# A fused infini-attention and MLP kernel whose hand-held order of 1,426 pieces of work is replaced by another

## The chip, the cores and the metric

The kernel runs on one core of one Trainium2 chip. The metric is the device time of one execution, in microseconds (us). The core has TensorE (PE in the profile), VectorE (DVE), ScalarE (ACT), GpSimd (POOL) and SyncE (SP, which here only issues DMAs). Each engine takes its instructions strictly in the order in which they stand in its queue; an instruction that waits for a semaphore holds up everything behind it on that engine.

## The reference

One transformer block on x of 2048 tokens by 640 features, in bfloat16: a layer norm, infini-attention with 32 heads of 20 features, a residual, a second layer norm, and an MLP with 1728 hidden features and SiLU, with a residual.

```
x = A_x
h  = x + A(layernorm(x))            # infini-attention
h2 = h + silu(layernorm(h) @ w1) @ w2

A(x):  q, k, v = x @ wq, x @ wk, x @ wv        # 32 heads x 20
  M = z = 0
  for s in range(4):                            # segments of 512 tokens
    p     = softmax(qs @ ks.T * 20**-0.5 + causal mask)
    a_dot = p @ vs
    a_mem = (phi(qs) @ M) / (phi(qs) @ z + 1e-6)    # phi(t) = t+1 if t > 0 else exp(t)
    out_s = g * a_mem + (1 - g) * a_dot             # g = sigmoid(beta)
    M, z  = M + phi(ks).T @ vs, z + sum(phi(ks))
  return concat(out_s) @ wo
```

## The kernel before

The work of the four segments is cut into 1,426 **tasks**, each a short run of instructions on one engine (a projection of a column block, one exp, one DMA). `build()` declares them all, `Graph.schedule()` puts them in one sequence, and they are emitted in that sequence into the engines' queues. A tracker follows who last wrote and read each buffer and sets the semaphore waits from that, so any sequence computes the same thing, and the sequence alone decides what an engine has next in its queue and what that has to wait for.

The sequence is a module-level table, `ORDER` (lines 356 to 460), a list of words of the form `name/engine:slots`. The name picks a task. The letter behind the slash picks the engine where a task may run on several: A is ACT, D is DVE, G is POOL, S is SP. The numbers behind the colon give the buffers that the task takes from the pools that it touches first, above all the **PSUM banks** (eight, 0 to 7): a score takes four neighbouring banks (`:4` is banks 4 to 7) or two, a V projection two, a projection or a part of the MLP one bank. A task that takes a bank waits for the last reader of what lay there. A `+` in the name of an exp makes one exp of 2048 columns out of two of 1024; `fill2` is a run of two matmuls on zeros, whose result nobody reads. What `schedule()` does with a word:

```
            name, _, slots = row.partition(":")
            name, _, eng = name.partition("/")
...
            t.eng = {"A": AC, "D": DV, "G": PO, "S": SP}[eng] if eng else list(t.engs)[0]
...
                    a.slot = slots.pop(0)
                    for k in range(a.slot, a.slot + a.size):
                        o = owner[a.pool][k]
                        assert o is None or o.users == 0, (name, a.pool)
```

The tasks by their names, with the line that shows up in the profile:

- **First norm**: n1_st, n1_r, n1_ap are statistics and normalisation of one block of 128 tokens; n1_tr4 to n1_tr15 are DMA transposes of the blocks of segments 1 to 3 into xT (L799, from SP); segment 0 goes over PE instead (L779).
- **Loads**: x0 to x14 (L576 ff.), the weights (L582); w_w1_0 to w_w1_4 are five pieces of w1.
- **Projections** (`declare_front`): pr (L867, in segment 0 also L872) into PSUM, qe is the copy of it to SBUF (L883, on ACT or DVE; the copies go into buffers that the trace calls w_sb in segment 0 and QK later). v00 to v03 are the V projections of the four 128-token blocks of segment 0 (L828, ten matmuls of 320 columns each), ve the copy into Vx (L842/L843), v10 to v13 those of segment 1. ex (L890) and pha, phb (L743 and others) make phi.
- **Virtual heads**: only four heads fit the rows of a 128-partition block at steps of 32, with 12 rows over in each step. Twelve small DMAs per segment, vt (L915), gather those rows of the q and k chunks into three more chunks, QKV (vt x0, x3, x6, x9 from chunks 0 to 2; the other eight from chunks 3 and 4). The scores of head groups 5, 6 and 7 read them. In segment 0 these copies are traced as w_sb<-w_sb. vp (of segments 1 and up) does the same for phi.
- **Scores** (L965): qk, row-tiled matmuls, four side by side, one for each head of a group of four, into four PSUM banks. Segment 0 is cut in halves of its queries: 0x1 to 0x3 are the first half of groups 0 to 3 on its own keys, packed into three scores, 4x1 to 4x3 that of groups 4 to 7 (4x3 is the one that the prediction calls the third score), 0y1 to 0y3 and 4y1 to 4y3 the second half on its own keys, 0ya to 7ya the second half of each group on the keys of the first. 0x1 and its like consist of a wide part and two narrow ones, 0x2 of two wide parts. 4x1 reads the virtual heads of group 5 beside group 4, 4x2 those of groups 5 and 6. qk8 to qk31 are segments 1 to 3. **Exps** (L977, ACT): e, named as their score. Masks mk (L988, POOL).
- **Attention output**: av (L1009, L1093), oe the copy of it, tn the transpose back (L1039, L1043, L1124), nm the division, ad the sum with the memory part, which together fill otok.
- **Memory**: kt (L1208) transposes phi(k), mz (L1226) multiplies it with V, ma (L1238) is the copy of the memory matrix Mz out of PSUM (ma00 the first one), mb copies the running matrix for the next segment.
- **Back** (`declare_back`): ot transposes otok into oT by DMA (L1265, from SP), wo0 to wo15 is the projection with wo (L1273), rs adds the residual (L1281), n2_ the second norm, h1 (L1308, tail L1302) the first MLP product by column blocks (h1_1_9 is block 9 of segment 1), th the tanh (L1317), s the rest of SiLU (L1323), h2 (L1350) the second product, o (L1363) the last residual, out (L1368) the store. bsel (L638) and zf (L649) are small preparations from beta on ACT.

PE works in two modes, whole-array matmuls (pr, v, mz, wo, h1, h2) and row- or column-tiled ones (qk, av, tn), and the order decides how often it changes.

Of the kernel before, what the change touches and what calls it, by code (L numbers as in the profile page):

```python
# [324 lines left out]
D = 640  # L325
# [31 lines left out]
epsg0:0 vpad0 zpad w2z/G:0 fill30:7 x0:0 w_q1:0 warm iota mt mta mtb mm7 x1:4 mm0 n1_st1/A:0,0 w_q0 w_q2 epsc sel  # L357
halfc n1_st0/D:5 n1_r0/G n1_r1/D n1_ap0:0 n1_tp0:4 n1_te0a/A:0 n1_ap1:1 n1_tp1:0 n1_te0b/A n1_te1b/D n1_te1a/A w_k0
re_wq1/D:0 pr010x:4 re_wq4/A re_wq2/D pr020x:2 qe020x/A:0 qe010x/A:0 re_wq3/D re_wq0/D pr000x:5 pr040x:6 w_k1
re_wk2/A:0 qe000x/A:0 re_wk1/D qe040x/A:0 pr011x:0 qe011x/A re_wk0/D pr001x:2 pr021x:5 qe001x/A qe021x/A x2:10,5  # L360
n1_st2/D:3 n1_r2/G qk0x10:0 pr030x:7 w_wv0:0 w_wv1 n1_st3/D:1 n1_r3/G e0x10:4 x4:2,1,11,3 qe030x/A:0 w_wo:0 beta
w_w1_0:0 e0x12 re_wk3/D pr031x:6 n1_ap2:2 re_wk4/D x8/S:6,7,8,9 n1_ap3:0 n1_tp2:0 n1_te2/D n1_st6:4 n1_tp3:4 n1_r6/G
n1_te3/A qe031x/D pr041x:7 qe041x/D qk0x20:0 e0x2+:6 pr030y:4 qe030y/D pr031y:5 qe031y/A pr041y:6 qe041y/A pr040y:7
qe040y/A vt02/S:0 vt011/S vt05/S vt08/S n1_st5:1 qk0x30:0 vt04/S mk0x1_0 mk0x1_256 n1_st4:5 n1_r5/G n1_ap5:1 e0x3+:0
n1_ap6:2 pr000y:4 qe000y/D lsc0 vt07/A pr021y:6 qe021y/D pr001y:5 qe001y/D pr011y:7 ex021:0 qe011y/D pr020y:1 n1_r4/D
mk0x3_0 qe020y/D mk0x3_256 vt010/A pr010y:6 qe010y/D vt00/A vt03/A vt06/S v03:2 ve03/D:0 ex001:1 mk0x3_384 mk0x2_0
v00:4 ve00/D qk0y10:0 e0y12:5 mk0x1_384 pha021:1 pha001:2 v01:6 e0y10 mk0y1_0 mk0x2_256 vt09/S phb021 vt01/S qk4x10:2
phb001 lsc1 n1_st7:7 e4x1+:2 vpad1 v02:0 ve01/D av0x:6 mk4x1_0 n1_ap4:3 n1_r7/G qk4x20:2 e4x2+:1 n1_tr5:0 mk4x1_256
mk4x1_384 ve02/D lsc2 lsc3 oe0x/D:0 mk4x2_0 mk4x2_256 av2x:7 ex041:1 oe2x/D:1 kt02:0 n1_tr6 mk0y1_256 mm2 kt00:1 v11:0
qk4x30:2 e4x30:3 pha011:0 ve11/D:1 tn0x:6 nm0x:3 e4x32 mk4x3_0 pha031:1 qk0ya0:0 mk4x3_256 n1_ap7:2 mk4x3_384 v12:6  # L370
e0ya+:4 w_w1_2 ve12/D av4x:4 oe4x/D:0 mz00:5 ma00/A:2,5 qk1ya0:0 e1ya2:0 tn2x:6 nm2x:0 av6x:7 oe6x/D:1 e1ya0 tn4x:6
nm4x:1 qk2ya0:2 kvz e2ya2:1 tn6x:7 mm3 nm6x:2 n1_tr4 v10:0 n1_st11:2 e2ya0 qk0y20:4 e0y2+:6 w_w1_3 w_w1_1 mk0y2_0
kg00/G:0 mk0y2_256 n1_tr7 v13:2 n1_r11/G qk3ya0:4 e3ya0:3 ve10/D n1_st9:6 n1_r9/D pha041:2 ex031:2 mm6 ve13/D ot1:0
wo1:0 n1_st8:3 e3ya2 ot0 ex011:0 wo0:2 rs1 n2_st1:0 mk0y1_384 w_w1_4 phb011 qk4ya0:4 e4ya0:2 n2_r1/D kg02/G e4ya2 rs0
n2_ap1:0 n2_st0:0 pr101:0 qe101/A:0 av0y:1 qk0y30:2 e0y3+:0 w_w2_0/S pr120:6 zf0 n2_r0/D oe0y/D:0 pr100:7 mk0y3_0
ex101:0 qk5ya0:2 n2_ap0:3 e5ya2:4 n2_tr1:0 phb041 qe100/D e5ya0 qe120/D:0 pr121:0 qe121/D qk4y10:4 mk0y3_256 tn0y:1
nm0y:3 e4y10:5 e4y12 mk0y3_384 n1_r8/D av2y:0 oe2y/D:1 qk6ya0:2 mk4y1_0 pha120:0 pr141:1 qe141/D:0 phb031 n2_tr0
h1_0_7_0:6 e6ya+:0 th0_7_0:0 s0_7_0:0 h1_0_12_0:0 th0_12_0:1 qk7ya0:1 e7ya+:1 kt01:0 w_w2_5 h1_0_4_0:7 tn2y:5 s0_12_0
h1_0_3_0:6 kg01/G mk4y1_256 n1_st10:1 th0_3_0:0 mk4y1_384 qvz h1_0_6_0:0 qk4y20:1 th0_4_0:1 nm2y:3 s0_4_0 mm4
h1_0_5_0:5 e4y2+:3 s0_3_0 pr110:7 qe110/D:0 th0_5_0:1 qk4y30:1 pr140:6 th0_6_0:0 e4y32:6 mk4y2_0 e4y30 w_w2_1/S  # L380
# [1046 lines left out]
```

## Time and profile before

| | before |
|---|---|
| median of 3 runs | 296.9 us (296.9 to 297.67) |
| the profiled execution: span | 296.3 us |
| its busy time, PE | 282.1 us (95%) |
| DVE / ACT / POOL | 222.2 / 217.3 / 140.0 us |
| instructions | 7,415 |

The page of the profile is one execution; its span runs from the first to the last instruction, 0.6 us less than the median of the runs. A view by windows gives, for each stretch, PE, PEld (weight loads), DVE, ACT and POOL busy time with the number of instructions, then the granted clock of PE, the busy share of the DMA engines and the GB/s. A timeline row reads: start, duration, engine, line, operation, output<-input, shape; xN joins N instructions alike that stand together, and the square bracket gives the idle time ahead of it and what ended it. In the view of waits a row gives the waiting instruction, the releaser, then the total, the number and the longest of such waits. Some matmul records are missing from the trace, so that a gap of about 0.2 us between matmuls need not be idle time.

### The profile page before, as it was taken

To read this page: it belongs to the slowest core of one execution; us is meant where nothing else is said; L and a number is where in the kernel's file an instruction comes from. 1 tells how busy PE (TensorE), PEld (TensorE's weight loads), DVE (VectorE), ACT (ScalarE), POOL (GpSimd) and SP (SyncE) were. 2 spreads that over 40 slices of the span, in tenths; PEclk is the share of its full clock that TensorE was granted. 3 is DMA by queue.
4 is the path that set the end of the run, shared out by engine and by line. 5 is a ranking of instruction groups with operands and counts; after the bars stand their busy time and mean duration, and the time that the engine had idled before them with its cause. 6 is when DMAs were issued, how large, how long until landed. Compare 5 with 4: busy or idle time off the path is not lost.

```text
span 296.3 us, 7415 instructions
## 1 busy us (share of the span) xinstructions
PE 282.1 (95%) x2968; PEld 167.6 (57%) x2991; DVE 222.2 (75%) x506; ACT 217.3 (73%) x266; POOL 140.0 (47%) x257
## 2 busy tenths in 40 slices
PE   7897889999999999999999999999999999999997
PEld 5675445555665455566643545465665457764575
DVE  3897799778979779899698967759967688626522
ACT  4884989999999899998879999788759750014400
POOL 6237735645566477646526646455476620200000
PEclk9999999999999999999999999999999999999999
DMA  7956973803953221255433400144171023220002
GB/s 243 367 173 105 173 133 71 221 18 75 189 94 74 53 60 22 40 109 106 104 96 61 66 1 2 27 76 87 22 99 32 0 61 74 68 67 25 22 22 91
DMA packets 49922, 25.40 MB, mean 86 GB/s; under 512 B 39504, under 2 KB 48048, under 8 KB 49888
## 3 DMA queue, kind: packets, MB, share of 16 engines
q1 hardware_dynamic: 47804, 22.69, 36.2%
q10 hardware_dynamic: 2084, 2.23, 2.4%
q8 instruction: 24, 0.39, 0.5%
q14 instruction: 10, 0.08, 0.1%
HBM read 10.41 MB, written 2.62 MB: 44 GB/s over the span
## 4 chain that ended last, share of the span: by engine, by line
PE 78%; DVE 8%; DMA 6%; issue 2%; ACT 2%; SPq 1%; POOL 1%; DVEq 0%; ACTq 0%
PE ps_all L1350 19%; PE ps_all L1308 17%; PE ps_all L867 12%; PE ps_all L965 7%; PE ps_all L1273 6%; PE ps_all L828 5%; PE ps_all L1009 5%; DMA x_tok<-in_A_x_dram 3%; DMA xT<-xn_rot 2%; ACT PT L977 2%; PE ps_all L1039 1%; DVE stt L743 1%; PE ps_all L1093 1%; DMA w_sb<-w_sb 1%; PE ps_all L1226 1%
## 5 line engine op out<-in xcount | busy, mean ns | idle before, releaser
L977 ACT ACTIVATE PT<-ps_all 128x1024 bf16<-128x1024 f32 (+1 forms) x120 | 153.2, 1310 | 16.9 <-PE ps_all L965 15.7
L988 POOL TENSOR_SCALAR_AFFINE_SELECT PT<-PT 128x512 bf16<-128x512 bf16 x128 | 81.6, 648 | 59.2 <-ACT PT L977 56.9
L1350 PE MATMUL ps_all<-w_sb,sT 128*128 128x320 bf16 (+2 forms) x462 | 64.9, 295 | 0.0
L1308 PE MATMUL ps_all<-hT,w_sb 128*128 128x512 bf16 (+1 forms) x315 | 61.0, 336 | 1.2 <-issue 0.6
L1317 ACT ACTIVATE th<-ps_all 128x512 f32<-128x512 f32 (+2 forms) x70 | 34.1, 505 | 35.3 <-PE ps_all L1308 31.2
L1350 PEld LDWEIGHTS ps_all<-w_sb,sT 128*128 128x128 bf16 x462 | 43.2, 98 | 18.3 <-issue 1.8
L1323 DVE SCALAR_TENSOR_TENSOR sT<-th,ps_all 128x512 bf16<-128x512 f32 (+2 forms) x70 | 37.9, 561 | 17.8 <-ACT th L1317 16.9
L1308 PEld LDWEIGHTS ps_all<-hT,w_sb 128*128 128x128 bf16 x325 | 29.9, 98 | 25.3 <-issue 3.5
L764 POOL TENSOR_TENSOR rst<-rst,eps_c 128x1 f32<-128x1 f32 x32 | 18.3, 576 | 24.4 <-DVE rst L758 23.1
L743 DVE BATCH_NORM_STATS2 stt<-x_tok 128x6 f32<-128x320 bf16 x62 | 27.2, 481 | 1.1 <-DMA x_tok<-in_A_x_dram 0.7
L1363 DVE SCALAR_TENSOR_TENSOR x_tok<-ps_all,x_tok 128x640 bf16<-128x640 f32 (+3 forms) x18 | 13.3, 745 | 16.7 <-PE ps_all L1350 16.6
L1071 POOL TENSOR_TENSOR otok<-on 128x320 bf16<-128x320 bf16 x24 | 19.0, 797 | 11.7 <-DVE on L1063 11.7
L1273 PE MATMUL ps_all<-wo_sb,oT 128*128 128x320 bf16 x160 | 23.8, 299 | 0.0
L884 DVE CAST QK<-ps_all 128x512 bf16<-128x512 f32 x23 | 15.7, 688 | 9.1 <-PE ps_all L867 8.9
L1063 DVE TENSOR_TENSOR on<-ps_all,rd 128x640 bf16<-128x640 f32 x24 | 19.8, 824 | 0.9
L828 PE MATMUL ps_all<-wv_sb,xT 128*128 128x320 bf16 x120 | 18.3, 299 | 1.1 <-DMA xT<-xn_rot 0.9
L1273 PEld LDWEIGHTS ps_all<-wo_sb,oT 128*128 128x128 bf16 x160 | 15.0, 98 | 7.2 <-issue 1.8
L867 PE MATMUL ps_all<-xT,wkr 128*128 128x512 bf16 x67 | 16.9, 379 | 1.2 <-issue 0.8
L867 PE MATMUL ps_all<-xT,wqr 128*128 128x512 bf16 x70 | 17.3, 380 | 0.4 <-issue 0.2
L1009 PE MATMUL ps_all<-PT,Vx 128*32 128x512 bf16 (+3 forms) x384 | 16.4, 301 | 0.1
L843 DVE CAST Vx<-ps_all 128x640 bf16<-128x640 f32 x15 | 12.3, 818 | 5.4 <-PE ps_all L828 5.3
L770 DVE TENSOR_SCALAR xn_rot<-x_tok,mvt,rst 128x640 bf16<-128x640 bf16 x32 | 14.9, 475 | 1.7 <-POOL rst L764 1.0
(106 smaller groups left out, 337.4 us busy)
## 6 DMA issues: line engine op xcount, KB each, us to landing
w_sb<-in_B_w_dram SPq DMA_DIRECT2D x5, 432.0 KB, 6.3
w_sb<-in_B_w_dram SPq DMA_DIRECT2D x3, 480.0 KB, 4.6
x_tok<-in_A_x_dram SPq DMA_DIRECT2D x2, 640.0 KB, 9.7
out_dram<-x_tok ACTq DMA_DIRECT2D x8, 160.0 KB, 1.8
out_dram<-x_tok SPq DMA_DIRECT2D x7, 160.0 KB, 1.9
x_tok<-in_A_x_dram SPq DMA_DIRECT2D x3, 320.0 KB, 3.4
QKV<-QK SPq DMA_DIRECT2D x12, 72.0 KB
wo_sb<-in_A_wo_dram SPq DMA_DIRECT2D x1, 800.0 KB, 10.4
```

The costliest lines, as they stand in the source:

```text
L743: T.add(DV, lambda e, hh=hh: e.bn_stats(out=stt[:, s, 6 * hh:6 * hh + 6], in_=xb[:, 320 * hh:320 * hh + 320]), reads=R((xa, xsub)), writes ...
L828: fns.append(lambda e, c=c, hh=hh: e.matmul(bank(ps, hh)[:, 0:320], lhsT=xT_[:, c, 128 * i:128 * i + 128], rhs=wv_sb[:, c, 320 * hh:320 * ...
L867: fns = [lambda e, kc=kc: e.matmul(bank(ps)[:, lo:hi], lhsT=wt[:, kc, c, :], rhs=xT_[:, kc, lo:hi], start=(kc == 0), stop=(kc == NC - 1)) ...
L965: fns.append(lambda e, j=j, o=o, r=r, q0=q0, q1=q1, qa=qa, ka=ka: e.matmul(ps_all[:, o:o + q1 - q0], lhsT=ka[32 * r:32 * r + DH, 128 * j:1 ...
L977: T.add(AC, lambda e: e.activation(out=pt[:, pta.slot, q0:q0 + nq, 0:width], in_=sc3[:, b0:b0 + nq, 0:width], func=ACT.Exp, scale=SCALE), ...
L988: T.add(PO, lambda e: e.affine_select(out=v, in_=v, pattern=[[0, 4], [1, 128]], compare_op=ALU.is_ge, fill=0.0, base=0, channel_multiplier ...
L1009: fns.append(lambda e, j=j, r=r, h=h, pa=pa, pt=pt, co=co, q0=q0, ji=ji: e.matmul(bank(po)[32 * r:32 * r + 32, q0:hi], lhsT=Vx[:, vx.slot, ...
L1273: fns.append(lambda e, c=c, hh=hh: e.matmul(bank(ps, hh)[:, 0:320], lhsT=oT[:, c, 128 * i:128 * i + 128], rhs=wo_sb[:, c, 320 * hh:320 * h ...
L1308: fns = [lambda e, c=c: e.matmul(bank(ps)[:, lo:hi], lhsT=w1_sb[:, c, 128 * f:128 * f + 128], rhs=hT[:, c, lo:hi], start=(c == 0), stop=(c ...
L1317: T.add(AC, lambda e: e.activation(out=th[:, tha.slot, lo:hi], in_=bank(ps)[:, lo:hi], func=ACT.Tanh, scale=0.5), reads=R((ps, [0])), writ ...
L1323: T.add(DV, lambda e: e.scalar_tensor_tensor(out=sT[:, f, lo:hi], in0=th[:, tha.slot, lo:hi], scalar=1.0, in1=bank(ps)[:, lo:hi], op0=ALU. ...
L1350: fns.append(lambda e, f=f, t0=t0, fr=fr, hh=hh, n=n: e.matmul(bank(pa, hh)[:, 0:n], lhsT=sT[:, f, t0:t0 + 128], rhs=w2_sb[:, fr, c0 + 320 ...
```

## The change

Only the table `ORDER` changes. Its first loads and norms stay nearly as they were; behind them the words stand in a new order, with other engines and other buffers for some. All 1,426 tasks are in both tables. Of the 381 tasks on PE, 198 stand at the same place in PE's queue. 21 copies go from DVE to ACT and 13 from ACT to DVE; 16 small tasks go from DVE to POOL and 11 back. 32 DMA issues (14 vt, 12 vp, two pieces of w2, x12, three stores) go from SP to ACT, 9 from ACT to SP. 40 exps are whole 2048-column ones in both. PE's mode changes are 195 before and 192 after. The filler of two matmuls that closed the program stands ahead of h1_2_4 instead, and the last piece of output has 192 columns instead of 128.

One line of the table around the V projections of segment 0, before and after:

```
-qe020y/D mk0x3_256 vt010/A pr010y:6 qe010y/D vt00/A vt03/A vt06/S v03:2 ve03/D:0 ex001:1 mk0x3_384 mk0x2_0
...
+n1_ap6:0 n1_ap7:1 vt02/A n1_ap5:2 vt04/S v03:2 v00:0 lsc0 lsc1 kvz ve03/D:1 vt01/A vt010/S lsc2 vt00/S mk0x3_0
```

On PE, at the V projections of segment 0 (L828, v03 first), before. The scores (L965) among them are 0y1 behind the first two, and 4x1; the L1093 rows are the attention output av0x, and the last row is score 4x2:

```order
L828 MATMUL ps_all<-wv_sb,hT 128x320 x20
L965 MATMUL ps_all<-w_sb 128x256 x4
L965 MATMUL ps_all<-w_sb 128x128 x8
L828 MATMUL ps_all<-wv_sb,hT 128x320 x10
L965 MATMUL ps_all<-w_sb 128x256 x4
L965 MATMUL ps_all<-w_sb 128x128 x8
L828 MATMUL ps_all<-wv_sb,hT 128x320 x10
L1093 MATMUL ps_all<-PT,Vx 32x256 x4
L1093 MATMUL ps_all<-PT,Vx 32x128 x4
L1093 MATMUL ps_all<-PT,Vx 32x256 x4
L1093 MATMUL ps_all<-PT,Vx 32x128 x4
L965 MATMUL ps_all<-w_sb 128x256 x8
```

The same place of PE after:

```order
L965 MATMUL ps_all<-w_sb 128x256 x4
L965 MATMUL ps_all<-w_sb 128x128 x8
L828 MATMUL ps_all<-wv_sb,hT 128x320 x40
L965 MATMUL ps_all<-w_sb 128x256 x8
L1093 MATMUL ps_all<-PT,Vx 32x256 x4
L1093 MATMUL ps_all<-PT,Vx 32x128 x4
```

Score 0y1 now stands ahead of all four V projections, these follow one another, and score 4x2 (the row of 8) comes ahead of 4x1, which stands behind four pairs of L1093 (av0x and av2x).

On ACT at the same place before; the exps (L977) are the two halves of 0y1, then 4x1 and 4x2 whole, and the DMAs (L915) are four of the twelve virtual-head copies:

```order
L915 DMA w_sb<-w_sb 8x2x1024
L890 ACTIVATE ex<-w_sb 128x512
L915 DMA w_sb<-w_sb 8x2x1024
L915 DMA w_sb<-w_sb 12x3x1024 x2
L890 ACTIVATE ex<-w_sb 128x512
L977 ACTIVATE PT<-ps_all 128x1024 x2
L977 ACTIVATE PT<-ps_all 128x2048 x2
```

And after, from behind four copies of projections (L883) on:

```order
L977 ACTIVATE PT<-ps_all 128x1024
L915 DMA w_sb<-w_sb 12x3x1024
L977 ACTIVATE PT<-ps_all 128x1024
L915 DMA w_sb<-w_sb 8x1x1024
L638 ACTIVATE bsel<-beta_bc 128x32
L915 DMA w_sb<-w_sb 8x2x1024
L649 ACTIVATE zf<-beta_bc 128x32
L842 ACTIVATE Vx<-ps_all 128x32x20
L890 ACTIVATE ex<-w_sb 128x512 x2
L977 ACTIVATE PT<-ps_all 128x2048
L890 ACTIVATE ex<-w_sb 128x512
L977 ACTIVATE PT<-ps_all 128x2048
```

The two exps of 0y1 now come first, with DMA issues between them and the two whole exps, of which 4x2's is the first; one of the copies of V (L842) and zf (L649) lie between.

On SP, at the transposes of segment 1 (L799; n1_tr4 and n1_tr7 are the last two of them) and the loads of w1 (L582), before:

```order
L582 DMA w_sb<-in_B_w_dram 128x1728
L799 DMA_TRANSPOSE xT<-xn_rot 128x5x128
L582 DMA w_sb<-in_B_w_dram 128x1728 x2
L799 DMA_TRANSPOSE xT<-xn_rot 128x5x128
L1265 DMA_TRANSPOSE oT<-otok 128x5x128 x2
```

And after:

```order
L1208 DMA_TRANSPOSE phiKt<-phiK 128x4x128
L582 DMA w_sb<-in_B_w_dram 128x1728
L1208 DMA_TRANSPOSE phiKt<-phiK 128x4x128
L799 DMA_TRANSPOSE xT<-xn_rot 128x5x128 x2
L1265 DMA_TRANSPOSE oT<-otok 128x5x128 x2
L582 DMA w_sb<-in_B_w_dram 128x1728
```

Only one piece of w1 stands ahead of the two transposes now; the two that stood between them come behind.

More of the change, by code (lines that the diff above doesn't have):

```diff
@@ L356 @@
 ORDER = """
[L357 removed]
+epsg0:0 vpad0 zpad w2z/G:0 fill30:7 x0:8 w_q1:0 warm iota mt mta mtb mm7 x1:7 mm0 n1_st1/A:0,0 w_q0 w_q2 epsc sel
 halfc n1_st0/D:5 n1_r0/G n1_r1/D n1_ap0:0 n1_tp0:4 n1_te0a/A:0 n1_ap1:1 n1_tp1:0 n1_te0b/A n1_te1b/D n1_te1a/A w_k0
[L359 to L360 removed]
@@ L371 @@
[L371 to L380, printed above, removed]
@@ new lines @@
+nm6x:3 n1_tr4 v10:0 ve10/D qk0y20:4 e0y2+:4 mzc0 n1_st9:1 v13:2 qk3ya0:4 ve13/D e3ya0:1 ot1:0 e3ya2 wo1:0 mk0y1_0
+mk0y1_256 mk0y1_384 ot0 qk4ya0:2 mzc1 e4ya2:2 mk0y2_0 w_w1_1 pha011:2 phb011 n1_r8/D mk0y2_256 rs1 n2_st1:6 n2_r1/D
+e4ya0 kg02/G kt01:1 w_w1_3 wo0:6 rs0 av0y:1 qk0y30:2 oe0y/D:0 e0y3+:5 n2_st0:4 pr101:6 w_w1_4 qe101/D:0 ex101:0 tn0y:1
+pr120:0 qk5ya0:2 e5ya2:3 n2_ap1:0 pr100:7 n2_tr1:0 qe120/D:0 n2_r0/G n2_ap0:1 mk0y3_0 mk0y3_256 mk0y3_384 n2_tr0 e5ya0
+pr121:0 ex031:2 qe100/D nm0y:2 qk4y10:4 e4y10:6 qe121/D e4y12 av2y:1 qk6ya0:2 e6ya+:0 w_w2_0/S n1_st10:6 pr141:0
```

180 lines of the change are left out of this document (93 added, 87 removed).

## The prediction

> **What bounds the kernel now.** I read the page first, then PE's waits, then windows by stage, then the timeline of the one stage that has room.
>
> ```profile
> span 296.3 us, 7415 instructions
> ...
> PE 282.1 (95%) x2968; PEld 167.6 (57%) x2991; DVE 222.2 (75%) x506; ACT 217.3 (73%) x266; POOL 140.0 (47%) x257
> ...
> PEclk9999999999999999999999999999999999999999
> ```
> PE is busy 95% at full granted clock all through. The change keeps every computation (one filler is placed elsewhere), so it can win only idle time of PE. Where is that idle time? PE's waits, all of them by cause (total, times, longest):
>
> ```profile
> PE ps_all L965 <- DMA w_sb<-w_sb: 1.5, 1, 1.5
> PE ps_all L872 <- DVE wqr L695: 1.2, 1, 1.2
> PE ps_all L620 <- DVE zpad L597: 1.1, 1, 1.1
> ...
> PE ps_all L779 <- DVE xn_rot L770: 0.9, 2, 0.6
> PE ps_all L965 <- DVE otok L1138: 0.9, 1, 0.9
> PE ps_all L828 <- DMA xT<-xn_rot: 0.9, 1, 0.9
> ```
> 1.1 (filler), 1.2 and 0.9 belong to the first loads and norms, whose order ahead of the projections stays. The other three large ones are 3.3 us. The windows say where they are (columns: PE, PEld, DVE, ACT, POOL busy):
>
> ```profile
> 20.00:48.00 28.00, 23.98 (x304) 15.18 (x303) 24.07 (x58) 21.47 (x23) 17.43 (x33) 1.00 0.69 128
> 48.00:80.00 32.00, 30.55 (x415) 17.97 (x418) 26.55 (x69) 31.73 (x42) 16.58 (x29) 1.00 0.52 112
> 80.00:150.00 70.00, 68.77 (x800) 40.54 (x805) 59.24 (x135) 62.91 (x74) 42.90 (x77) 1.00 0.38 74
> ```
> Between 20 and 48 us PE idles 4.0 us. Between 48 and 80 us it idles 1.45 us and ACT only 0.27: there **ACT sets the pace**, and PE can come earlier only if ACT does. From 80 us PE's waits, asked for alone, name two that are more than issue, 0.4 and 0.3 us:
>
> ```profile
> PE ps_all L1226 <- DVE x_tok L1281: 0.4, 1, 0.4
> PE ps_all L1308 <- DVE rd L1057: 0.3, 1, 0.3
> ```
> So the time is decided before 80 us, and in 20 to 48 us above all.
>
> **Stage 20 to 48 us.** These rows are PE's, ACT's and two DMAs' of that stage:
>
> ```profile
> 22.29 2.88 PE L828 MATMUL ps_all<-wv_sb,hT 128*128 128x320 bf16 x20
> 25.11 0.40 PE L965 MATMUL ps_all<-w_sb 20*128 20x256 bf16 x12
> 28.47 0.40 PE L965 MATMUL ps_all<-w_sb 20*128 20x256 bf16 x12 [1.50 <-DMA w_sb<-w_sb]
> 33.23 0.40 PE L965 MATMUL ps_all<-w_sb 20*128 20x256 bf16 x12
> 42.68 1.53 PE L828 MATMUL ps_all<-wv_sb,xT 128*128 128x320 bf16 x10 [0.85 <-DMA xT<-xn_rot]
> 47.85 1.03 PE L867 MATMUL ps_all<-xT,wkr 128*128 128x512 bf16 x4 [0.16 <-DVE stt L743]
> ```
> ```profile
> 18.28 0.93 ACT L883 ACTIVATE w_sb<-ps_all 128x256 bf16<-128x256 f32 x3
> 19.12 1.88 ACT L977 ACTIVATE PT<-ps_all 128x2048 bf16<-128x2048 f32 x1
> 21.36 3.34 ACTq L915 DMA_DIRECT2D w_sb<-w_sb  x3
> 24.75 0.63 ACT L890 ACTIVATE ex<-w_sb 128x512 bf16<-128x512 bf16 x1 [2.76 <-DVE Vx L843]
> 28.92 1.88 ACT L977 ACTIVATE PT<-ps_all 128x2048 bf16<-128x2048 f32 x1 [1.43 <-PE ps_all L965]
> 31.30 1.88 ACT L977 ACTIVATE PT<-ps_all 128x2048 bf16<-128x2048 f32 x1 [0.50 <-PE ps_all L965]
> 41.88 1.88 ACT L977 ACTIVATE PT<-ps_all 128x2048 bf16<-128x2048 f32 x1 [0.21 <-PE ps_all L965]
> 44.59 1.02 ACT L977 ACTIVATE PT<-ps_all 128x1024 bf16<-128x1024 f32 x1 [0.84 <-PE ps_all L965]
> ```
> ```profile
> 23.78 0.78 SPq L915
> 24.60 3.73 DMA w_sb<-w_sb
> ...
> 35.73 6.91 DMA xT<-xn_rot
> ```
> Before, the score of group 4 (28.47) waits 1.50 us for the last virtual-head copy, issued at 24.60 and landed 3.73 later. The change puts all four V projections and one early score (qk0y1) ahead of it, and score 4x2 ahead of 4x1. I follow it by hand.
>
> Step 1: qk0y1 needs ACT's copies of the projections. ACT ends its exp at 19.12 + 1.88 = 21.0, then has one ex (0.63) and four copies, which start 0.27 apart (18.28: three in 0.93, one is 0.38); the third frees qk0y1 at about 22.8, the fourth ends at 23.05. PE loses 0.4 there. Step 2: one V projection takes (25.11 - 22.29)/2 = 1.4 less a switch, 1.36; the score and four of them end at 22.8 + 0.35 + 5.45 + 0.1 = **28.7**. Step 3: the virtual-head copies of the first three chunks become issuable at 23.05; three on SP at about 0.8 each end at 25.5, and landing takes 3.73 - 0.70 = 3.03 from the issue's end: 28.5. So 4x2 starts at 28.7 and **the 1.50 us wait goes**, with 0.2 us to spare. Step 4: what is late next is ACT. Before, one 1.88 us exp (28.92) ran beside PE's V projection and the second ended at 33.18; now both lie behind 28.7. 4x2's exp is 28.7 + 0.45 (28.92 - 28.47) = 29.15 to 31.03; 4x1 shares two PSUM banks with 4x2 (slots 4 and 2, four banks each), waits for that end, and its exp is 31.55 to 33.43. The third score starts at 33.5, where it started at 33.23: **0.25 late**. The early end of V is given back. Step 5: behind it both kernels run the same exps; moving the Mz copy from ACT to DVE takes away 0.3, and the V projection that now must wait for its PSUM pair costs about 0.3. The exp of 41.88 comes 0.3 late. Step 6: n1_tr4 and n1_tr7 now go ahead of two w1 loads on SP, so the 6.91 us landing shortens and the **0.85 us wait goes**; but the next score needs the banks of the 41.88 exp, which ended at 43.76, and ACT's idle before 44.59 was 0.84. Of that, the 0.3 is made up; wo0 then waits for the PSUM of exp 3ya2. The set of PE work done at 47.62 (0.22 ahead of the row at 47.85, whose first matmul's record is lost) is reached at about 47.85: **+0.25 us**. The 3.3 us of waits are nearly all replaced by ACT's chain.
>
> What a change of tiling mode costs:
>
> ```profile
> 101.46 1.24 PE L867 MATMUL ps_all<-xT,wqr 128*128 128x512 bf16 x5
> 102.63 0.40 PE L965 MATMUL ps_all<-QKV 20*128 20x512 bf16 x4
> 102.96 1.25 PE L867 MATMUL ps_all<-xT,wkr 128*128 128x512 bf16 x5
> ```
> Four row-tiled matmuls take 0.33 where one of 512 columns takes (1.24 - 0.38)/4 = 0.215: 0.11 a change. PE changes mode 195 times before and 192 after, all three fewer ahead of 48 us. [...] I take 0, since in this stage PE waits for ACT anyway.
>
> **Stage 48 to 80 us.** ACT loses one copy (qe101, now DVE's) and zf0, and gets ex031 (0.63): even. The early exp at 50 us does not help: tn0y is put ahead of score 4y1, PE reaches that later, and the exps behind are paced by it: **+0.1**.
>
> **From 80 us.** The filler of two matmuls moves from behind the last output to ahead of h1_2_4, on PE's path: 0.2 us (bounds 0 if PE waits there, 0.38 by its row). The last output part is 192 columns instead of 128: 0.36 for 0.29, **+0.07**.
>
> ```profile
> 293.44 0.36 DVE L1363 SCALAR_TENSOR_TENSOR x_tok<-ps_all,x_tok 128x192 bf16<-128x192 f32 x1 [0.89 <-PE ps_all L1350]
> 293.80 0.38 PE L620 MATMUL ps_all<-zpad 128*128 128x256 bf16 x2
> 294.00 0.29 DVE L1363 SCALAR_TENSOR_TENSOR x_tok<-ps_all,x_tok 128x128 bf16<-128x128 f32 x1 [0.20 <-PE ps_all L1350]
> ```
> Of the waits from 80 us the 0.3 (h1_1_9, whose bank was mz20's) goes, as mz20 is moved ahead; I leave the 0.4: **-0.3**. New waits there are unknown: 0 to +1.0 (a handful of 0.2 each, the size of those found now), taken as 0.
>
> **DMA issues.** 32 go from SP to ACT and 9 back. Covered, they cost nothing: the one at 190.42 took 0.72 inside an exp.
>
> ```profile
> 190.36 1.88 ACT L977 ACTIVATE PT<-ps_all 128x2048 bf16<-128x2048 f32 x1 [0.20 <-PE ps_all L965]
> 190.42 0.72 ACTq L915 DMA_DIRECT2D QKV<-QK  x1
> ```
> Uncovered they do: three at 21.36 took 3.34, and ACT idled 2.76 before 24.75. Nearly all new ones stand behind an exp of 1.0 to 1.9, so I take 0; bounds 0 and 23 x 0.72 = 17 of ACT.
>
> **The sum** against the profiled execution: +0.25 + 0.1 + 0.2 + 0.07 - 0.3 = +0.3 on 296.3. The median of the runs, 296.9, lies 0.6 above that span: **297.2 us**.
>
> **The rivals.** (a) *The late landings are the bound, and ACT follows.* If step 4's ACT chain is shorter than I make it (qk0y1 frees at 22.4, 4x2 at 28.3), 0.4 less there, 0.4 at step 5, none of the 0.25, and half of the 0.85 kept: about -1.6, **295.3**. For it: three waits of 3.3 us do go. Against: ACT's 0.27 us of idle from 48 to 80. [...] Chance 0.28. (b) *The landing is late after all.* Slower: place, score 4x2; it decides once the last copy lands after 28.7, since then both exps and everything to 80 us move with it, one for one. One further issue (0.8) and a landing 0.4 slower (3.4) make +1.2: **298.4**. Chance 0.18. (c) *ACT's issues block*: from 48 to 150 us thirteen of the moved ones stand on ACT; if three are uncovered at 0.72, +2.1: **299.3**. Chance 0.08. That the order has no effect at all is excluded: the queues stand as the table says.
>
> **Chances.** Forecast 0.46 (own range 296.3 to 298.1). A measurement of this kernel can tell 0.3%, 0.9 us, from no change. Faster by that is most of (a) and a little of the forecast: 0.30. Slower is (b), (c) and the forecast's upper end, where unknown waits from 80 us add: 0.28. The rest, 0.42, is within. The range 294.6 to 299.0 takes in the forecast, (b), and (a) with the mode changes' 0.3 and the 0.4 of the L1226 wait gained as well (295.3 - 0.7).
>
> **What would show it.** In the changed profile PE's waits must no longer name w_sb or xT DMAs; 4x2's score should start near 28.7 and the third at 33.5; ACT must be solid from 50 to 80 us; waits from 80 us should stay under 1 us. Wrong it is if 4x2 starts after 29.5 (b), if the third score starts before 33.0 (a), or if ACT shows idle time beside its own DMA issues (c).

## The result, and the profile after

| | before | changed |
|---|---|---|
| median | 296.9 us (296.68 to 297.67) | 301.31 us (300.23 to 303.26) |
| ratio to before | 1 | 1.0146, 95% interval 1.0103 to 1.0189 |
| profiled execution: span, granted clock | 296.3 us, 1.000 | 299.9 us, 0.994 |

The changed kernel is 1.5% slower; 297.2 us was predicted, and the range ended at 299.0. From the page of the changed kernel:

```profile
span 299.9 us, 7422 instructions
...
PE 287.5 (96%) x2991; PEld 168.8 (56%) x2991; DVE 218.3 (73%) x493; ACT 220.6 (74%) x274; POOL 140.6 (47%) x262
...
PEclk9999979999999999999999999999999999999999
```

PE's busy time is 5.4 us more than before though its work is nearly the same: 23 of its matmuls had no record before (2,968 of 2,991), and a slower clock stretches others here (v10 below takes 2.82 us at a granted clock of 0.50). In the sixth fortieth of the span (37.5 to 45 us) the clock's digit is 7; before, it was 9 all through. The windows (PE, PEld, DVE, ACT, POOL busy, granted clock, DMA share, GB/s) put that in the stage that the prediction worked through, and show that ACT is no longer solid behind it:

```profile
20.00:48.00 28.00, 23.51 (x290) 14.25 (x287) 21.32 (x52) 21.99 (x27) 17.40 (x33) 0.94 0.47 95
48.00:80.00 32.00, 31.06 (x422) 17.93 (x423) 25.88 (x62) 30.38 (x38) 15.67 (x31) 1.00 0.58 135
```

PE's waits by cause:

```profile
PE ps_all L965 <- ACT PT L977: 3.8, 7, 1.2
...
PE ps_all L1308 <- DMA hT<-xn_rot: 0.5, 1, 0.5
PE ps_all L965 <- DMA w_sb<-w_sb: 0.4, 1, 0.4
```

The wait for the virtual-head copies fell from 1.5 to 0.4 us and the one for xT is gone. In their place scores wait 3.8 us for ACT's exps, a cause that was not in the list before. PE's timeline of the stage (start, duration, and in brackets the idle time ahead):

```profile
22.34 0.40 PE L965 MATMUL ps_all<-w_sb 20*128 20x256 bf16 x12 [0.20 <-ACT w_sb L883]
22.67 5.61 PE L828 MATMUL ps_all<-wv_sb,hT 128*128 128x320 bf16 x40
28.72 0.40 PE L965 MATMUL ps_all<-w_sb 20*128 20x256 bf16 x8 [0.44 <-DMA w_sb<-w_sb]
...
31.10 0.40 PE L965 MATMUL ps_all<-w_sb 20*128 20x256 bf16 x12 [1.18 <-ACT PT L977]
...
33.48 0.40 PE L965 MATMUL ps_all<-w_sb 20*128 20x256 bf16 x12 [0.52 <-ACT PT L977]
...
37.80 0.40 PE L965 MATMUL ps_all<-w_sb 20*128 20x256 bf16 x8 [0.91 <-ACT PT L977]
...
40.40 2.82 PE L828 MATMUL ps_all<-wv_sb,xT 128*128 128x320 bf16 x10
...
43.56 1.53 PE L828 MATMUL ps_all<-wv_sb,xT 128*128 128x320 bf16 x10
...
48.14 1.52 PE L1273 MATMUL ps_all<-wo_sb,oT 128*128 128x320 bf16 x10 [0.34 <-ACT PT L977]
```

Up to 33.48 the stage runs as forecast. Then one V projection, v10 at 40.40, takes 2.82 us where its like at 43.56 takes 1.53. Nothing waits in it: PE's granted clock is 0.50 there, from 39.94 to 43.35 us (the windows are under e13).

### The profile page after: what moved, and what is told of

It is laid out like the page before. It is cut to its first block, busy times and chain, and to the rows that moved or that the text cites. A ratio compares the mean times of both kernels' runs of the same rounds, so it can differ in the third digit from the quotient of the medians.

```text
span 299.9 us, 7422 instructions
## 1 busy us (share of the span) xinstructions
PE 287.5 (96%) x2991; PEld 168.8 (56%) x2991; DVE 218.3 (73%) x493; ACT 220.6 (74%) x274; POOL 140.6 (47%) x262
## 4 chain that ended last, share of the span: by engine, by line
PE 75%; ACT 11%; DVE 5%; DMA 4%; issue 2%; SPq 2%; ACTq 0%
PE ps_all L1350 18%; PE ps_all L1308 16%; PE ps_all L867 11%; ACT PT L977 9%; PE ps_all L1273 7%; PE ps_all L965 7%; PE ps_all L828 5%; PE ps_all L1009 4%; PE ps_all L620 2%; DMA x_tok<-in_A_x_dram 2%; SPq L915 1%; DMA w_sb<-w_sb 1%; DMA hT<-xn_rot 1%; PE ps_all L1039 1%; ACT th L1317 1%
## 5 line engine op out<-in xcount | busy, mean ns | idle before, releaser
L977 ACT ACTIVATE PT<-ps_all 128x1024 bf16<-128x1024 f32 (+1 forms) x120 | 153.0, 1310 | 18.9 <-PE ps_all L965 17.6
L1308 PE MATMUL ps_all<-hT,w_sb 128*128 128x512 bf16 (+1 forms) x325 | 62.9, 337 | 0.5 <-DMA hT<-xn_rot 0.5
L828 PE MATMUL ps_all<-wv_sb,xT 128*128 128x320 bf16 x120 | 19.6, 313 | 0.5 <-DVE on L1063 0.2
L867 PE MATMUL ps_all<-xT,wkr 128*128 128x512 bf16 x75 | 18.7, 380 | 0.0
L867 PE MATMUL ps_all<-xT,wqr 128*128 128x512 bf16 x75 | 18.4, 380 | 0.0
L884 DVE CAST QK<-ps_all 128x512 bf16<-128x512 f32 x21 | 14.4, 686 | 4.6 <-PE ps_all L867 4.4
L1281 DVE TENSOR_TENSOR x_tok<-ps_all,x_tok 128x640 bf16<-128x640 f32 x16 | 13.0, 813 | 5.6 <-PE ps_all L1273 5.3
```

Of the source, the lines that this page charges most:

```text
L828: fns.append(lambda e, c=c, hh=hh: e.matmul(bank(ps, hh)[:, 0:320], lhsT=xT_[:, c, 128 * i:128 * i + 128], rhs=wv_sb[:, c, 320 * hh:320 * ...
L867: fns = [lambda e, kc=kc: e.matmul(bank(ps)[:, lo:hi], lhsT=wt[:, kc, c, :], rhs=xT_[:, kc, lo:hi], start=(kc == 0), stop=(kc == NC - 1)) ...
L977: T.add(AC, lambda e: e.activation(out=pt[:, pta.slot, q0:q0 + nq, 0:width], in_=sc3[:, b0:b0 + nq, 0:width], func=ACT.Exp, scale=SCALE), ...
L1308: fns = [lambda e, c=c: e.matmul(bank(ps)[:, lo:hi], lhsT=w1_sb[:, c, 128 * f:128 * f + 128], rhs=hT[:, c, lo:hi], start=(c == 0), stop=(c ...
```

## The experiments

Every time is a median beside runs of the kernel before on the same chip; e1 to e4 ran on one chip, e5 to e8 on another, e9 to e11 on a third, e12 to e15 on the first, so that across these groups the ratios to before are to be compared. **Theory T**: the halved clock follows a stretch in which PE did little, and it is part of the loss. **Rival A**: ACT's late chain of exps alone sets the time. **Theory L**: the rest is lost behind 50 us, to late landings.

### The same program twice (e13)

The changed kernel again, without an edit.

> The changed kernel itself once more, for the count of halved stretches beside the next run on the same chip. Theory T: most executions at 0.994 or 0.989, each such stretch 1.3 to 1.5 us, the others near 300.2; median 301.

301.36 us, ratio 1.0136 (1.0101 to 1.0170). Seven executions: 299.25 and 301.06 us at clock 1.000, four of 300.79 to 302.20 at 0.994, one of 302.20 at 0.989. With the first four, 8 of 11 executions of this kernel had a halved stretch; of the 93 of the kernel before that stood beside the experiments, 3 had. The profiled execution is the one of 299.25 us, without a halving. Its PE timeline:

```profile
37.80 0.40 PE L965 MATMUL ps_all<-w_sb 20*128 20x256 bf16 x8 [0.90 <-ACT PT L977]
...
40.39 1.52 PE L828 MATMUL ps_all<-wv_sb,xT 128*128 128x320 bf16 x10
...
46.76 1.52 PE L1273 MATMUL ps_all<-wo_sb,oT 128*128 128x320 bf16 x10 [0.34 <-ACT PT L977]
```

From score 4x2 (28.71 and 28.72) up to v10 the two executions agree to 0.01 us; there one loses 1.30 us, and wo0 starts 1.38 us later. That is the price of one halving here, free of every other difference. Why only one of them? The windows, first of the profiled changed kernel, cut at the edges of its clock, then of this execution, whose clock fell only behind its end, at 298.2 us, cut in steps counted back from there:

```profile
36.53:39.94 3.41, 2.17 (x52) 1.28 (x50) 3.04 (x9) 2.85 (x3) 2.09 (x5) 1.00 0.03 7
39.94:43.35 3.41, 3.41 (x25) 1.72 (x22) 1.50 (x5) 2.14 (x3) 1.44 (x3) 0.50 0.18 34
```

```profile
35.39:38.80 3.41, 2.40 (x61) 1.48 (x64) 2.78 (x7) 2.85 (x3) 2.04 (x4) 1.00 0.25 50
38.81:42.22 3.41, 2.96 (x50) 1.56 (x38) 2.76 (x9) 3.27 (x4) 2.22 (x5) 1.00 0.01 2
```

The halving lasts 3.41 us. In the two profiled executions whose clock fell twice, the falls lie whole multiples of that apart. In e7 (below) they lie at 33.33 and 43.57 us, 10.24 apart, 3 times 3.413:

```profile
33.33:36.74 3.41, 3.24 (x22) 1.64 (x22) 0.07 (x1) 2.51 (x3) 1.90 (x3) 0.50 0.88 196
...
43.57:46.98 3.41, 3.41 (x26) 1.90 (x18) 1.65 (x5) 2.44 (x3) 1.72 (x4) 0.50 0.03 6
```

In e4 (below) they lie at 39.97 and, behind the end, at 299.4 us, 76 times 3.413 apart. From these I take a grid of 3.413 us within an execution; that e13 has it too is an estimate, as its clock fell only once. Counted back from 298.2 us, 76 steps, the grid cuts its weak stretch at 38.8 us: the window ahead of the cut holds only the wait of 0.90 us, and the one behind it the wait of 0.34 us and v10. In the profiled changed kernel one window holds both waits, and PE was busy for 2.17 of its 3.41 us.

The busy share does not tell the cases apart. In the same changed execution an earlier window had PE busy for less, and full clock followed:

```profile
29.70:33.12 3.42, 2.08 (x34) 1.12 (x22) 1.93 (x5) 3.42 (x3) 2.26 (x5) 1.00 0.51 108
```

So I estimated the time in which PE streamed columns: 0.42 ns a column, from the 0.215 us that the prediction works out for 512, from the starts of all matmuls, overlaps once. In the four windows of the program that were followed by a halving (in the changed kernel, e4, and twice in e7) it was 1.18 to 1.43 us of 3.41. The lowest at full clock that were not followed by one, in the changed kernel and in e13, had 1.63 to 1.70. Whether there is a limit between 1.43 and 1.63 is not shown, and the count was chosen with the halvings known: another count might separate them as well.

### Matmuls of nothing in PE's waits (e1, e9)

```
-... phb021 oe2x/D:1 qk4x10:2 ... tn2x:4 w_w1_2 qk1ya0:0 ...
+... phb021 oe2x/D:1 fill10:3 qk4x10:2 ... tn2x:4 w_w1_2 fill8:7 qk1ya0:0 ...
```

> The changed kernel with eighteen matmuls of nothing more: eight fillers where PE waits 0.91 us for an exp at 36.9 us, ten where it waits 1.18 us ahead of score 4x1 at 29.9 us; nothing else is touched. Theory T (the halved clock from 40.0 to 43.4 us follows a stretch in which PE did little, and costs about 1.3 us, V10 2.82 us instead of 1.53): the added work keeps the clock at 1.00, so the mean clock is 0.998 or more in nearly every execution and the time falls by about 1.3 us to 300.0, though work was added. Rival A (ACT's chain alone sets the time; the clock is a side effect): no gain, 301.3, or up to 0.3 later where a filler runs over the wait. If the clock still falls, what counts as activity is not whole-array matmuls, or the drop has another cause.

301.01 us, 1.0132 (1.0113 to 1.0151), and clock 1.000 in all four executions: 0.3 us less than the changed kernel, not 1.3. T was right on the clock and wrong on the whole time. In the stretch itself the price is gone. Score 0x2, ahead of it, and exp 4y2, behind it, stand in the profile of e1 at

```profile
16.66 0.40 PE L965 MATMUL ps_all<-w_sb 20*128 20x256 bf16 x8
...
62.48 1.88 ACT L977 ACTIVATE PT<-ps_all 128x2048 bf16<-128x2048 f32 x1
```

The 45.82 us between them are 47.23 in the profiled changed kernel and 45.95 in e13. But score 0x2 starts 0.93 us later than in the changed kernel, behind a wait ahead of all fillers, and from exp 4y2 to the end another 0.2 us is lost:

```profile
9.16 0.70 PE L867 MATMUL ps_all<-hT,wqr 128*128 128x256 bf16 x5 [1.67 <-DVE wqr L695]
```

The start differs from execution to execution: score 0x2 stands between 15.37 and 16.66 us in the 17 profiles, late and early ones with either order. Whether the other three executions of e1 began late too, no trace shows. The same words in the kernel of e4 (head of the changed table, order of before behind 50 us):

> The kernel with the head of the changed table and the rest of before, with the same eighteen matmuls of nothing in PE's two waits of its head. Without them it took 298.3 to 298.8 in executions at clock 1.000 (3 of 7) and 299.8 to 302.2 in those with one or two halved stretches (4 of 7). Theory T: all executions at clock 1.000 and all near 298.5, median 1.2 us lower than without the added work. Rival (the fillers cost as much as the clock gives, as the 301.0 of the changed kernel with them hints): clock 1.000, but 299.5.

298.54 us, 1.0052 (1.0033 to 1.0070), against 299.79, 1.0088 (1.0055 to 1.0121), without them. All executions at clock 1.000. From the profile of e9, where the eight matmuls stand in place of the wait of 0.91 us:

```profile
37.52 1.04 PE L620 MATMUL ps_all<-zpad 128*128 128x256 bf16 x8
38.59 0.40 PE L965 MATMUL ps_all<-w_sb 20*128 20x256 bf16 x8
```

The medians differ by 1.25 us, as T says. The intervals of the ratios overlap, so the gain is likely and not shown; the executions of e4 at full clock (298.28 to 298.79 us, below) lie where e9 does. With the fillers (e1, e9, e12, e14) no execution of 28 was halved, where 8 of 11 of the changed kernel and 4 of 7 of e4 were. In e1 PE also has a new wait of 0.4 us at 90 us (tn8, told under e14).

### A wait filled in the kernel before (e2)

```
-... qk4x30:2 e4x30:3 ... ve11/D:1 tn0x:6 nm0x:3 ... qk0ya0:0 ... v12:6 ... av4x:4 oe4x/D:0 ...
+... qk4x30:2 v12:6 e4x30:3 ... ve11/D:1 ... qk0ya0:0 ... av4x:4 tn0x:6 nm0x:3 oe4x/D:0 ...
```

> The kernel before with one V projection of segment 1 (v12) moved ahead of score 0ya, into PE's wait of 0.9 us at 33.6 us, and the transpose tn0x behind it, as the changed kernel has it. Nothing else. Theory T: behind it, from 35.4 to 39.9 us, nothing of size is left for PE, so a stretch of 3.4 us with little work comes about as in the changed kernel; in some or most executions the mean clock reads 0.994 and the time is 1.3 us longer, 298.2. Rival A: ACT sets the pace there (it is solid from 31 to 42 us), so filling the wait changes nothing, 296.9, clock 1.000; the naive sum says 0.3 to 0.9 faster.

297.5 us, 1.0016 (0.9996 to 1.0036). Nine executions at clock 1.000 have a median of 297.22, within 0.2 of before; three at 0.994 took 298.21, 299.01 and 299.17. So a wait of 0.87 us of PE, filled with its own later work, gained nothing: in its place PE waits for ACT's exps, 0.94 us in two waits.

```profile
35.27 0.51 PE L1093 MATMUL ps_all<-PT,Vx 128*32 128x256 bf16 x16 [0.34 <-ACT PT L977]
...
36.95 0.40 PE L965 MATMUL ps_all<-w_sb 20*128 20x256 bf16 x8 [0.60 <-ACT PT L977]
```

And the clock was halved in 3 of 12 executions. The profiled one is not among them, so that the place of the halving is not shown. A is right on the wait, T on the clock.

### Which part of the order (e3, e4, e5, e6)

The words of one table up to a point, then the others in the order of the other table; some SBUF slots, and in e6 one PSUM bank, had to be others.

```
e3 = before[:294] + rest of changed          e5 = before[:294] + changed[:1002] + rest of before
e4 = changed[:296] + rest of before          e6 = before[:1006] + rest of changed
```

> The first 294 words of the table before (to about 50 us), behind them the changed table's order. If the loss lies in the head (clock 1.3 and ACT's chain 0.5), this is 1.7 to 2.0 us faster than the changed kernel and 1.5 to 1.9 slower than before: 298.6, clock 1.000. If the loss lies behind 50 us (DMA issues on ACT, late landings), it stays at 300 to 301.

298.68 us, 1.0068 (1.0040 to 1.0096); 7 of 8 executions at clock 1.000.

> The first 296 words of the changed table, behind them the order of before. The mirror of the last: if the head carries the loss, 296.9 + 1.7 to 2.0 = 298.6 to 298.9 in executions with one halved stretch, clock 0.994; without one, about 297.4. If the loss lies behind 50 us, 297 whatever the clock.

299.79 us, 1.0088 (1.0055 to 1.0121). By the clock: 298.28, 298.57 and 298.79 at 1.000; 299.79, 300.10 and 300.68 at 0.994; 302.15 at 0.989. Each halving costs about 1.6 us. Head and rest each carry a part: 1.5 us of the head at full clock, 1.7 us behind it. That the part behind is late landings isn't shown by this.

> Order of before up to about 50 us, of the changed table from there to about 176 us (its first 1,002 words), of before again from there. The kernel with the head of before and all the rest changed was 1.7 us slower than before. If those 1.7 us are many small waits spread over the rest, half of them are here: 297.8. If they are a late transpose at 223 us, the filler and the tail (theory L), this one is within 0.5 us of before: 297.0 to 297.5. Clock 1.000 in either case.

298.28 us, 1.0039 (1.0027 to 1.0052): 1.3 slower than before, above both forecasts (the interval's lower end is 297.8).

> Order of before up to about 176 us, of the changed table from there. Theory L (the transpose n2_tr8 that lands 0.7 us late ahead of h1_2_7, the filler 0.2, the tail about 0.3): 1.0 to 1.3 us slower than before, 298.0 to 298.3. Spread over the rest: 297.8.

299.21 us, 1.0071 (1.0047 to 1.0095); two of six at 0.994, the other four 298.41 to 299.70. Middle and late part together (e3) cost 1.7, alone 1.3 and 1.5 or more: the pieces don't add up. Each cut through the order makes a wait that neither whole kernel has, so that a part of these times is the cut's: 0.88 us at 54.87 us in e5, 0.66 at 57.00 in e4, 0.78 at 185.67 in e6, and in e3

```profile
54.03 0.95 PE L1093 MATMUL ps_all<-PT,Vx 128*32 128x256 bf16 x32 [0.87 <-DVE rst L758]
```

That the rest is one late transpose is refuted; that it is evenly spread isn't shown either.

### The stage of the V projections alone (e7)

```
e7 = before[:up to v03] + changed[:296] without those + rest of before
```

> Order of before up to the V projections (22 us), of the changed table from there to about 50 us (four V projections in a row, score 4x2 ahead of 4x1), of before again from there. If this stage carries what the head costs beside the clock (step 4 of the prediction, the early end of V given back because ACT's chain starts late), an execution at clock 1.000 takes 0.5 to 1.5 us more than before, 297.5 to 298.5, and those at 0.994 1.5 us more than that. If the first 22 us carry it, executions at clock 1.000 stay at 297.0; if the waits that the change removes (1.5 and 0.85 us) were a gain, 295 to 296.

303.43 us, 1.0204 (1.0182 to 1.0225); four of five executions at 0.989. The two orders don't fit at this cut: PE waits 2.0 us for an exp ahead of a score and 1.7 ahead of a V projection, which neither kernel does. So it says nothing on step 4. It shows the clock once more, two halvings in one execution, each behind a weak stretch (PE busy for 1.54 and 2.02 us of the 3.41 ahead):

```profile
PEclk9999788999999999999999999999999999999999
```

### A transpose sent first (e8)

```
-... e28e2 vp310/S h2_7_0:6 n2_ap9:1 ... n2_tr9 ... n2_tr8 h1_2_7_0:0 ...
+... e28e2 h2_7_0:6 n2_ap9:1 ... n2_tr9 ... n2_tr8 vp310/S h1_2_7_0:0 ...
```

> The kernel with the head of before and the rest of the changed table, with one DMA issue (vp310) moved from ahead of the transposes n2_tr9 and n2_tr8 to behind them on SP. Theory L: n2_tr8 goes out up to 0.7 us sooner, PE's wait of 0.7 us ahead of h1_2_7 shrinks, and the time falls by 0.4 to 0.7 from 298.7 to 298.0 to 298.3. Rival: n2_tr8 waits for its own input (n2_ap8, which ends at 221.4 us in the changed kernel), not for SP; then nothing changes, 298.7.

298.69 us, 1.0052 (1.0037 to 1.0067), beside 298.68, 1.0068 (1.0040 to 1.0096), without the edit. In the profile the wait is gone. From PE's waits of e3:

```profile
PE ps_all L1308 <- DMA hT<-xn_rot: 0.7, 1, 0.7
```

In e8 this row is missing, but so it is in e13, which has the order of the changed kernel untouched. This landing is late in some executions only. The times show no gain.

### Waits taken out of the kernel before (e10, e11, e15)

```
-... vt010/A pr010y:6 qe010y/D vt00/A ... vt09/S phb021 vt01/S ...
+... vt010/A pr010y:6 qe010y/D vt01/A vt00/A ... vt09/S phb021 ...
```

> The kernel before with one of the twelve virtual-head copies (vt01, the last that SP issues, at 24.60 us) issued by ACT instead, in ACT's idle time between 22.06 and 22.95 us. SP's last copy is then issued at 23.78, ACT's at 23.81. Theory: the wait of score 4x1 for its last copy (1.50 us in the profile of before) is what starts ACT's chain of exps, so the copy landing 0.8 us sooner brings the whole chain to 80 us forward: 296.2, 0.6 to 0.8 faster. Rival (PE's waits are not the bound, ACT's work is; or the landing itself takes longer with two queues at once): 297.0.

296.94 us beside 297.22, ratio 0.9991 (0.9978 to 1.0003): unclear. The copy's wait is 0.88 us instead of 1.50:

```profile
27.42 0.40 PE L965 MATMUL ps_all<-w_sb 20*128 20x256 bf16 x12 [0.88 <-DMA w_sb<-w_sb]
```

In the profile the chain comes forward by it: from score 0x2 to exp 4y2 it is 44.24 us, 45.20 before. Of that 0.3 us arrives in the median, and the interval holds the theory's lower end (0.998) as well as no gain. e11 moves `ma00` and `qe101` to DVE and `zf0` ahead on top of it, as the changed table does:

> The last kernel with three small pieces of ACT's work taken off its solid stretch from 31 to 80 us, as the changed table does: the copies ma00 and qe101 to DVE, zf0 ahead to 24 us. ACT loses 0.3 + 0.6 + 0.2 = 1.1 us of work there. Theory: ACT sets the pace there, so 0.5 to 1.0 faster than the last kernel, 295.3 to 295.7. Rival: DVE, 26.6 of 32 us busy there, is late in turn, and nothing is gained: 296.2.

297.75 us, 1.0026 (1.0007 to 1.0044): slower. Scores now wait for DVE, two waits that e10 does not have:

```profile
PE ps_all L965 <- DVE QK L884: 1.2, 1, 1.2
...
PE ps_all L965 <- DVE stt L743: 1.0, 1, 1.0
```

The first stands at 54.4 us: score 4y1 waits for a bank that a copy of DVE's (L884, qe120) empties, and that copy now stands behind qe101 on DVE. The second is in e15 too, which does not have these moves. The prediction had counted them as ACT's gain alone (0.3, and "even"). e15 is e10 with `mz10:0 ma10` moved behind `pr220:6`, the larger of the two waits from 80 us on, both of which the changed order removed:

> The kernel before with two small edits: vt01 issued by ACT (as in the run that came out at 0.999 of before) and the matmuls mz10 behind the projection pr220, as the changed table has it, so that PE does 1.2 us of work where it waited 0.4 us at 93.7 us. If PE's waits count from 80 us on (the changed kernel gained 0.35 us at this place), 0.6 to 0.7 us faster than before, ratio 0.998; if the wait only moves on (mz10's copy is then late on DVE), 0.999 to 1.000 as without it.

297.29 us, 1.0013 (0.9990 to 1.0036): nothing gained. No version that is shown to beat both kernels came of it.

### The last copy, and the sum (e12, e14)

```
-... n1_ap7:1 vt02/A ... vt06/S vt09/S ...
+... n1_ap7:1 vt09/A ... vt06/S vt02/S ...
```

> The kernel with the changed head, added matmuls and the rest of before, with two virtual-head copies exchanged: vt09 (a large one, which SP issued last, at 24.45 to 25.23 us in the changed kernel) goes to ACT at 23.7 us, vt02 (a small one) to SP's last place. Score 4x2 waited 0.44 us for SP's last copy, which landed 3.46 us after its issue ended, where the prediction had taken 3.03. Theory C (the landing of the large last copy makes the head late beside the clock): the wait goes, 0.3 to 0.5 faster, 298.1. Rival (the copies share the landing queues, the last of either engine lands at the same time): no change, 298.5.

299.02 us, 1.0052 (1.0033 to 1.0071), and the wait grew:

```profile
PE ps_all L965 <- DMA w_sb<-w_sb: 0.8, 1, 0.8
```

The ratio is that of e9, the same kernel without the exchange. Theory C falls. What sets the last landing stays open.

> The changed kernel with all that has been named undone: the eighteen added matmuls in its two waits (clock, 1.3), the exchange of vt09 and vt02 (0.4), the DMA issue vp310 behind the transposes (0.6), the filler of two matmuls back at the end (0.2). The sum is 2.5 us: 298.8, all executions at clock 1.000, 1.8 slower than before still, which would be ACT's late chain in the head and small waits. If the terms overlap, it stays above 299.5; if the late chain was the clock's doing too, 297.5.

301.22 us, 1.0128 (1.0091 to 1.0165), no halving in six executions. The sum is refuted: nothing is gained over the changed kernel, though the clock holds. One place can be named. DVE in e14, then in e13, at the copy of a transposed phi (L1199):

```profile
87.89 0.20 DVE L1199 COPY phiKv<-phiKt 128x128 bf16<-128x128 bf16 x1 [1.46 <-DMA phiKt<-phiK]
```

```profile
85.89 0.19 DVE L1199 COPY phiKv<-phiKt 128x128 bf16<-128x128 bf16 x1
```

The transpose lands late, DVE stands in order behind its copy for 1.46 us, the residual (L1281) behind that is late, and PE waits for it:

```profile
PE ps_all L1039 <- DVE x_tok L1281: 0.9, 1, 0.9
```

e1 has the same row with 0.4; the changed kernel has none. Why this landing is late with the fillers wasn't tried.

## Why the prediction was wrong

**What held.** Steps 1 to 4 hold almost to the hundredth: score 4x2 at 28.72 (28.7 forecast), the third score at 33.48 (33.5), and ACT's two whole exps, forecast at 29.15 and 31.55:

```profile
29.16 1.88 ACT L977 ACTIVATE PT<-ps_all 128x2048 bf16<-128x2048 f32 x1 [1.76 <-PE ps_all L965]
...
31.55 1.88 ACT L977 ACTIVATE PT<-ps_all 128x2048 bf16<-128x2048 f32 x1
```

Part of that is luck: V began at 22.67 instead of 23.2 and the last copy was late instead, a wait of 0.44 us that step 3 had excluded by 0.2. Step 6 held as well: the xT wait is gone, and wo0 waits for the PSUM of exp 3ya2 (0.34). That the removed waits are replaced by ACT's chain held, and e2 shows it for another.

**Two steps failed, and neither is the whole loss.** The three executions of the changed kernel without a halved stretch took 299.25, 300.23 and 301.06 us, all above 299.0; the other eight took 300.79 to 303.26.

**The first: "it can win only idle time of PE".** I read the clock of before, 1.00 all through, and took it as a constant. The order decides it too: it puts v12 ahead of score 0ya, the move that e2 makes alone, and leaves a stretch from 35.5 to 40.4 us in which PE has only tiled and narrow matmuls and waits 0.91 and 0.34 us for ACT. A halved clock (0.50 for 3.41 us in the profile) comes in 8 of 11 executions. That term, 1.3 us in the trace and about 1.6 by e4, was missing from the sum and from the rivals.

**The second: new waits from 80 us, "taken as 0".** This is the largest term, 0.9 to 1.9 us from 61 us on in the two profiles of the changed kernel, and its cause stays open (below).

**A term of the right sign, too small: ACT's chain.** I had +0.25 at the end of the head and +0.1 to 80 us. To measure it without the clock: score 0x2 (the first row) and exp 4y2 (the second) in before, in e3 with the head of before, in e13, and in the profiled changed kernel:

```profile
16.05 0.40 PE L965 MATMUL ps_all<-w_sb 20*128 20x256 bf16 x8
...
61.25 1.88 ACT L977 ACTIVATE PT<-ps_all 128x2048 bf16<-128x2048 f32 x1
```

```profile
15.37 0.40 PE L965 MATMUL ps_all<-w_sb 20*128 20x256 bf16 x8 [0.18 <-DVE hT L792]
...
60.35 1.88 ACT L977 ACTIVATE PT<-ps_all 128x2048 bf16<-128x2048 f32 x1
```

```profile
15.62 0.40 PE L965 MATMUL ps_all<-w_sb 20*128 20x256 bf16 x8
...
61.57 1.88 ACT L977 ACTIVATE PT<-ps_all 128x2048 bf16<-128x2048 f32 x1
...
295.14 0.36 DVE L1363 SCALAR_TENSOR_TENSOR x_tok<-ps_all,x_tok 128x192 bf16<-128x192 f32 x1 [0.86 <-PE ps_all L1350]
```

```profile
15.73 0.40 PE L965 MATMUL ps_all<-w_sb 20*128 20x256 bf16 x8
...
62.96 1.88 ACT L977 ACTIVATE PT<-ps_all 128x2048 bf16<-128x2048 f32 x1
...
297.51 0.36 DVE L1363 SCALAR_TENSOR_TENSOR x_tok<-ps_all,x_tok 128x192 bf16<-128x192 f32 x1 [0.86 <-PE ps_all L1350]
```

From one to the other it is 45.20, 44.98, 45.95 and 47.23 us. At full clock the changed head is 0.75 to 0.97 late, not 0.35; the clock adds 1.28. In absolute time exp 4y2 comes 0.32 late in e13 (61.57, 61.25 before), which looks like the 0.35; that is luck, as the profiled execution of before came to score 0x2 0.43 us later. ACT was not solid from 50 to 80 us either (30.38 of 32 us): score 0y3 stands behind wo0 and the attention output av0y, so ACT waits for PE there.

```profile
50.93 1.88 ACT L977 ACTIVATE PT<-ps_all 128x2048 bf16<-128x2048 f32 x1 [1.10 <-PE ps_all L965]
```

**From 61 us to the end.** The last residual ends at 294.00 + 0.29 = 294.29 before, at 295.50 in e13, at 297.87 in the changed kernel: from exp 4y2 on 233.04, 233.93 and 234.91 us. So 0.9 to 1.9 us are lost, where I had 0.2 + 0.07 - 0.3 and 0 to +1.0 for new waits, taken as 0. More profiles bear it out: the same distance is 232.7 to 233.4 us in the eight with the order of before in that part (before, e2, e4, e9 to e12, e15), and 233.9 to 235.5 in the six with the changed order (it, e1, e3, e8, e13, e14). The waits that the list names from 62 us on explain less than half, 1.6 us in the profiled changed kernel beside 0.9 before. About half of the spread between the two changed executions is the transpose ahead of h1_2_7, which lands late in some; the rest I can't put down to single places.

**The sum as measured**, for the two profiled executions from score 0x2 to the last residual: 0.75 (head) + 1.28 (clock) + 1.87 (rest) = 3.90, and 282.14 - 278.24 = 3.90. The first 16 us ran 0.3 sooner, which makes the 3.6 of the spans. The medians lie 4.4 apart, since the profiled execution of before was one of the slower ones of its kernel.

**The base.** The time of an execution lies 1.7 to 1.9 us above its span in all runs that give both (301.62 and 299.9, 299.25 and 297.5), not 0.6, and the 93 executions of before beside the experiments have a median span of 295.4 us, not 296.3. The two errors cancel in the forecast, which counts from the median of before.

**A reading.** The 0.11 us "a change" of tiling mode is for two, one into the tiled mode and one out of it, by the rows that it is worked out from; what one change costs by itself no run shows. The sum took 0 for it. The range counted 0.3 for three changes fewer, and no run shows that term either: in the changed kernel, with the three fewer, scores wait 3.8 us for ACT's exps.

**The rivals.** (c), issues that block ACT from 48 us on, is not seen: in the profiled changed kernel ACT's waits from 48 to 150 us name PE. Its sign shows once ahead of that, 0.69 us of ACT's idle time before zf at 25.55 us, behind two issues; it cost nothing, as ACT's next exp then waited 1.76 us for PE. (b), the landing late after all, came with 0.44 instead of 1.2. (a) is refuted by 33.48.

## What to carry to other kernels

Look at where PE's work of size stands, not only at how long PE waits: here, in a stretch of tiled and narrow matmuls and waits alone (35.5 to 40.4 us), the clock fell to half at 39.94 us for 3.41 us, and eighteen matmuls of nothing in two of PE's waits were a cheap test of it (no halving in 28 executions, against 8 of 11). Filling a wait of 0.87 us of PE brought nothing where another engine's chain set the pace (e2, ratio 1.0016); follow that chain first. One profile is one execution: the two of the changed kernel differ by 2.4 us, by the clock and by landings that were late in one of them, so run the same program again before a difference of that size is explained.

## What the runs showed of the hardware that was not expected

- PE's clock was halved (0.50) for 3.41 us in the profiled changed kernel, although in the 3.41 us ahead PE never waited for longer than 0.91 us and was busy for 2.17 us by the profile. The estimated time of streamed columns told the cases apart (1.18 to 1.43 us of 3.41 ahead of a halving, 1.63 to 1.70 in the lowest windows without one), and PE's busy time did not (2.17 us ahead of a halving, 2.08 without one).
- Whether a stretch is halved does not follow from the program alone: of two executions of the changed kernel, alike to 0.01 us from 28.7 to 40.4 us, one was halved from 39.94 to 43.35 us and the other (e13) stayed at 1.00.
- With eighteen matmuls on zeros the clock stayed up in 28 of 28 executions, without them in 6 of 18 (the changed kernel and e4), so matmuls on zeros were enough.
